# A long convolution with a spectral mixer: where the matrix of the modes is loaded

## The chip, the cores and the metric

The kernel runs on one core of a Trainium2 chip. The metric is the device time of one execution in microseconds (us); lower is better. Three runs of the kernel before took 382.86, 383.96 and 384.25 us, so the median is 383.96 us.

## The reference

What must be computed is a causal convolution over the sequence, followed by a mixer of 64 frequencies and a gated residual, for 8 batches of 5696 positions with 128 channels:

```python
def _attn_ref(x, h):                       # long convolution by FFT of twice the length
    L = 2 * S
    Yf = np.fft.rfft(x, n=L, axis=1) * np.fft.rfft(h, n=L, axis=0)[None, :, :]
    return np.fft.irfft(Yf, n=L, axis=1)[:, :S, :]

def _moe_ref(x, w_r, w_i, w_ch):
    X = np.fft.rfft(x, axis=1)             # only the first 64 frequencies are mixed
    Yr = einsum('bmd,mde->bme', Xr, w_r) - einsum('bmd,mde->bme', Xi, w_i)
    Yi = einsum('bmd,mde->bme', Xr, w_i) + einsum('bmd,mde->bme', Xi, w_r)
    u = x + np.fft.irfft(Y, n=S, axis=1)
    return u + np.maximum(u @ w_ch, 0.0)
```

## The kernel before

The transforms are matrix products. The sequence is split as 89 blocks of 64 positions. A first product over the 89 blocks gives 90 frequencies `k` (0 to 89) for each of the 64 places within a block; a second product, with the matrix `M`, transforms over the places; the result is multiplied with the filter's spectrum `Hs`; a third product, with `Wc`, goes back over the places, and its result `Zs` is stored to a scratch tensor in HBM. Much later a last stage loads it again, adds the mixer's part and writes the output.

The kernel writes out by hand, engine by engine, the order of all instructions: a recorder (class `Recorder`) takes each operation with the names of what it reads and writes, finds the semaphores that it must wait for, and appends it to its engine's list. Each engine, and each queue that issues transfers, works through its own list in order. All loads and stores named here are issued by SP (constants, `Hs`, `G`, stores of `Zs`) or by POOL (x, h and `M`).

The 8 batches are worked on in 4 pairs. The stages that matter here are:

- The tiles of the first pair (the loop over `a_tile(j, ...)` for j = 0 to 31, L668 to L674). Each tile is 8 matmuls of x (`Xin`) with the 90 frequencies and an eviction into `As`. Between them stand the 23 steps of the filter, `filter_tick(t, ...)` (L457), each for four frequencies: up to 16 matmuls of the filter's first transform `Ah` with `M`, and an eviction into `Hs`. After the steps 1, 5, 11, 17 and 22 (`HEND`), two transfers on SP copy the finished part of `Hs` from one half of the partitions to the other.
- The ticks of the first pair (`tick(g_, t)`, L646), t = 0 to 22, again of four frequencies each. A tick does `second` (matmuls with `M`), `products` (the multiplication with `Hs` on DVE, after an eviction by ACT), `third` of the tick two before (matmuls with `Wc`, eviction by ACT into one of ten buffers `Zs`/`Zt`, a 256 KB store to HBM issued by SP) and `modes_of` of the tick three before: small matmuls of `Zs` with `G`, which collect the 64 modes in one PSUM bank (the modes' matrix is `G`).
- In the ticks 2, 4, ... 16 a pair other than the last also issues the loads of the next pair's x (`x_load`, two transfers on POOL, 36 and 320 KB, into `Xt`), and in the ticks 9, 10, 13, 14, 17, 18, 20 and 22 (`XPLACE`) DVE copies what has landed into `Xin` (`x_place`, L356).
- After the ticks the tiles of the next pair follow, then its ticks, and so on.

`G` has 46 column groups of 128 (`NS`), one for each odd frequency and one that holds all even frequencies. It lies where `Ah` lay: group s takes the room of frequency s of `Ah`. It is loaded in six parts (`NG`) of eight groups (`GP`), five of 256 KB and one of 192 KB. A part may land only when the matmuls that read the same eight frequencies of `Ah` are done (the `after` of L480), and these belong to two steps of the filter. So in the kernel before `filter_tick` issues part i right behind step 2i + 1 (L477 to L480), on SP, behind any copy of `Hs` that the same step issues.

The matmuls of `modes_of` need part 0 from the first of them on (tick 3), and part i from frequency 16i - 1 on, whose `modes_of` stands in tick 4i + 2: part 1 in tick 6, part 2 in tick 10, part 5 in tick 22.

PE's instructions are not all on the chip at the start: while the kernel runs, a DMA queue of its own (q8 in the profile, "instruction") brings them in packets of 16 KB, over the same DMA engines.

## The time and the profile before

| | |
|---|---|
| median of three runs | 383.96 us |
| the profiled execution's own time | 384.32 us |
| its span, from the first to the last instruction | 382.2 us |
| mean granted TensorE clock | 0.988 |
| PE busy | 362.2 us (95%) |
| DVE busy | 307.4 us (80%) |
| ACT busy | 304.0 us (80%) |
| DMA queue q1 (issued by SP) | 67.73 MB, 51.5% of the 16 engines' time |
| DMA queue q0 (issued by POOL) | 35.43 MB, 44.2% |
| DMA queue q8 (instructions) | 42 packets, 0.69 MB, 0.7% |
| `G`: six issues on SP | 33.0 to 41.3 us, 9.8 to 11.8 us from issue to landing |
| `M`: six issues on POOL | 10.7 to 13.3 us, 18.1 to 28.7 us to landing |
| copies of `Hs` on SP | ten issues, 31.7 to 53.2 us, 3.5 to 11.7 us to landing |
| x for the second pair: 16 issues on POOL | 59.0 to 83.9 us, 2.7 to 7.2 us to landing |

Times within the execution count from its first instruction. The filter's steps run from 30.2 to 52.3 us, the first pair's ticks from 53.6 to about 93 us. "DMA share" is the mean busy share of the core's 16 DMA engines, where a value around 1 means that all are occupied all the time (packets can overlap a little, which gives values above 1). "issue" as the reason of an idle engine is time in which it waited for no semaphore that the profile shows.

### The profile page before, as it was taken

The page shows a single profiled execution, that of the slowest core. Times are in us where ns is not written, and L with a number is a line of the kernel's source. Part 1 is how long each engine was busy: PE and PEld are TensorE (multiplying, and loading weights), DVE is VectorE, ACT ScalarE, POOL GpSimd, SP SyncE. Part 2 cuts the span into 40 slices and gives each one's busy share as a digit, 9 for nine tenths or more (in the row PEclk, how much of TensorE's full clock was granted, in tenths as well). Part 3 has the DMA queues.
Part 4 walks back from the last instruction along what each step waited for, and adds up shares of the span by engine and source line. Part 5 has one row for each costly group of instructions (what it writes and reads, how often), then busy time and mean ns, then how long its engine had stood idle before and what let it go on. Part 6 is the DMA issues. An engine that isn't in the chain of part 4 may idle for free.

```text
span 382.2 us, 12483 instructions
## 1 busy us (share of the span) xinstructions
PE 362.2 (95%) x5372; PEld 284.0 (74%) x5372; DVE 307.4 (80%) x334; ACT 304.0 (80%) x497; POOL 81.9 (21%) x133
## 2 busy tenths in 40 slices
PE   7999789999989999989999899999999999989994
PEld 7998666666866667856667766668898988877873
DVE  6879678998998998989998888766347776766876
ACT  1269579999989998989998899994566777766785
POOL 8400003230652220832313010429100000000000
PEclk9999899999999999999999999998999999999998
DMA  7999978999899997999996379999999999999869
GB/s 146 195 282 370 239 180 159 242 240 276 89 150 204 234 255 213 119 131 235 246 272 144 39 238 365 322 328 383 397 406 403 409 401 411 409 399 377 346 267 358
DMA packets 83985, 103.94 MB, mean 272 GB/s; under 512 B 22062, under 2 KB 68910, under 8 KB 80450
## 3 DMA queue, kind: packets, MB, share of 16 engines
q1 hardware_dynamic: 59643, 67.73, 51.5%
q0 software_dynamic: 24288, 35.43, 44.2%
q8 instruction: 42, 0.69, 0.7%
q14 instruction: 12, 0.10, 0.1%
HBM read 70.61 MB, written 51.12 MB: 319 GB/s over the span
## 4 chain that ended last, share of the span: by engine, by line
PE 78%; ACT 9%; DMA 5%; DVE 5%; issue 2%; SPq 0%; DVEq 0%
PE ps L320 78%; ACT As L310 7%; DMA ZT0b<-zscr 5%; DVE As L314 2%; DVE U L594 1%; ACT R L832 1%; ACT UT L308 1%; DVE O L833 1%; DMA F<-cF 0%; DVE UT L312 0%; ACT XT L310 0%; SPq L317 0%; PE ps L786 0%; DVE Os L833 0%; DVEq L105 0%
## 5 line engine op out<-in xcount | busy, mean ns | idle before, releaser
L320 PE MATMUL ps<-U,Wc 128*128 128x512 f16 (+1 forms) x368 | 94.4, 376 | 0.0
L602 DVE TENSOR_TENSOR U<-Xs,Hs 128x2048 f16<-128x2048 f16 (+1 forms) x68 | 80.6, 1188 | 10.7 <-ACT Xs L308 9.6
L308 ACT CAST Xs<-ps 128x1024 f16<-128x1024 f32 (+1 forms) x72 | 69.5, 971 | 7.0 <-PE ps L320 4.8
L833 DVE TENSOR_TENSOR O<-ps,R 128x512 f32<-128x512 f32 x81 | 52.5, 686 | 22.1 <-ACT R L832 14.7
L308 ACT CAST Zs<-ps 128x512 f16<-128x512 f32 (+1 forms) x126 | 66.1, 605 | 0.0
L832 ACT ACTIVATE R<-ps 128x512 f32<-128x512 f32 x96 | 51.0, 573 | 16.0 <-PE ps L320 15.5
L314 DVE TENSOR_SCALAR As<-ps 128x720 f16<-128x720 f32 x64 | 53.5, 880 | 8.5 <-PE ps L320 7.2
L320 PE MATMUL ps<-F,Xin 128*128 128x180 f16 x512 | 54.6, 253 | 4.3 <-issue 2.6
L310 ACT ACTIVATE As<-ps 128x720 f16<-128x720 f32 (+1 forms) x68 | 49.0, 773 | 11.9 <-PE ps L320 10.7
L320 PEld LDWEIGHTS ps<-F,Xin 128*128 128x128 f16 x512 | 46.1, 156 | 11.4 <-DVE As L314 3.1
L320 PE MATMUL ps<-WI,UT 128*128 128x256 f16 x360 | 52.0, 279 | 1.8 <-DVE O L833 1.7
L320 PE MATMUL ps<-As,M 64*128 64x128 f16 x1440 | 48.6, 217 | 4.5 <-DVE U L594 3.5
L320 PEld LDWEIGHTS ps<-U,Wc 128*128 128x128 f16 x368 | 28.2, 97 | 28.9 <-ACT Zs L308 6.8
L320 PEld LDWEIGHTS ps<-As,M 64*128 64x128 f16 x1440 | 40.3, 94 | 10.3 <-DVE U L594 4.2
L317 POOL DMA_DIRECT2D Xt<-in_x_dram x48 | 25.0, 525 | 104.7 <-PE ps L320 104.0
L602 DVE TENSOR_TENSOR U<-ps,Hs 128x2048 f16<-128x2048 f32 x20 | 45.7, 2284 | 0.0
L308 ACT CAST UT<-ps 128x712 f16<-128x712 f32 x40 | 30.0, 752 | 18.3 <-PE ps L320 17.3
L320 PEld LDWEIGHTS ps<-WI,UT 128*128 128x128 f16 x360 | 39.2, 152 | 5.7 <-ACT R L832 2.6
L320 PE MATMUL ps<-IBs,C 128*128 128x356 f16 x128 | 39.9, 321 | 0.7
L320 PEld LDWEIGHTS ps<-G,Zs 128*128 128x128 f16 x492 | 27.0, 96 | 12.6
L308 ACT CAST Zt<-ps 128x512 f16<-128x512 f32 (+1 forms) x58 | 31.0, 605 | 0.0
L320 PE MATMUL ps<-G,Zs 128*128 128x2 f16 (+2 forms) x492 | 30.3, 191 | 0.0
(87 smaller groups left out, 503.8 us busy)
## 6 DMA issues: line engine op xcount, KB each, us to landing
out_dram<-O SPq DMA_DIRECT2D x39, 512.0 KB, 11.8
zscr<-Zs SPq DMA_DIRECT2D x60, 256.0 KB, 6.9
Xt<-in_x_dram POOLq DMA_DIRECT2D x24, 320.0 KB, 6.9
zscr<-Zt SPq DMA_DIRECT2D x28, 256.0 KB, 6.3
W<-wscr POOLq DMA_DIRECT2D x4, 1024.0 KB, 7.7
M<-cM POOLq DMA_DIRECT2D x5, 720.0 KB, 20.5
ZT0a<-zscr SPq DMA_DIRECT2D x3, 1024.0 KB, 15.1
Xr<-in_x_dram POOLq DMA_DIRECT2D x8, 320.0 KB, 14.0
```

Source lines behind the costliest of these rows:

```text
L308: R.add(e, lambda h_: h_.copy(dst, src), reads, writes, after=after)
L310: R.add(e, lambda h_: h_.activation(dst, src, COPY, scale=scale), reads, writes, after=after)
L314: R.add(e, lambda h_: h_.tensor_scalar_mul(dst, src, scale), reads, writes, after=after)
L317: R.add(eng, lambda h_: h_.dma_start(dst, src), reads, writes, ring=ring, after=after)
L320: R.add("tensor", lambda h_: h_.matmul(o, l, r, start=st, stop=sp), reads, writes)
L594: R.add("vector", lambda e, b=b, s_=s_: e.tensor_tensor(bass.AP(u_s[i], b * 512, [[2048, P], [1024, 2], [1, n * D]]), s_, hv, MULT), [tok, ...
L602: R.add("vector", lambda e: e.tensor_tensor(uv, src, hv, MULT), bk + [("h", t, 0), ("h", t, 1, 0), ("h", t, 1, J)], [("u", i)])
L832: R.add("scalar", lambda e: e.activation(rv, src_r, RELU), bk, [("r", i % NR)], after=once(("r", i % NR), G_ALL + XTT + [("y", 0), ("y", 1 ...
L833: R.add("vector", lambda e: e.tensor_tensor(ov, src_u, rv, ADD), bk + [("r", i % NR)], [key + (h_,)], after=once(key, old))
```

## The change

The six loads of `G` leave `filter_tick` and become a function `load_g(i)` with the same transfer, the same queue (SP), the same ring of semaphores and the same condition on `Ah`. It is called in the loop over the ticks: in the first pair, ahead of the ticks 0, 2, 4, 6, 8 and 10.

```diff
@@ filter_tick
-        if t % 2 and t // 2 < NG:
-            s0, s1 = t // 2 * GP, min(t // 2 * GP + GP, NS)
-            dma("sync", g_sb[:, s0 * P:s1 * P], bass.AP(c_g, s0 * P, [[GW, P], [1, (s1 - s0) * P]]), "c", (),
-                [("g", t // 2)], after=[("ag", k) for k in range(s0, s1)])
+
+    def load_g(i):
+        s0, s1 = i * GP, min(i * GP + GP, NS)
+        dma("sync", g_sb[:, s0 * P:s1 * P], bass.AP(c_g, s0 * P, [[GW, P], [1, (s1 - s0) * P]]), "c", (),
+            [("g", i)], after=[("ag", k) for k in range(s0, s1)])
...
     for g_ in range(NP):
         for t in range(NT + LM if g_ + 1 == NP else NT):
+            if g_ == 0 and t % 2 == 0 and t // 2 < NG:
+                load_g(t // 2)
             tick(g_, t)
```

The lists of PE, DVE, ACT and POOL hold the same instructions in the same order as before. On SP the ten copies of `Hs` now stand one after another; parts 0 and 1 of `G` follow behind the last of them, ahead of the first store of `Zs`; then two stores, part 2, two stores, part 3, two stores, part 4, two stores, part 5, and the remaining stores.

## The prediction

> **What bounds the kernel now.** I began with the chain of work that ended last, since it says what each stretch of the 382.2 us is made of, and looked at the two stages that the change touches.

> ```profile
> 2.58 31.37 PE ps L320 x416
> ...
> 33.97 7.91 PE ps L320 x190
> 41.88 2.58 issue
> 44.46 4.53 PE ps L320 x82
> ...
> 55.52 37.69 PE ps L320 x580
> ```

> The columns are start, length and what. PE is on the path nearly throughout, but at 41.88, in the stage in which `G` is loaded, there is a hole of 2.58 us with no semaphore behind it. PE's timeline shows that it is no wait of a tile: a tile is eight matmuls on one PSUM slot, and here it breaks off after six.

> ```profile
> 41.19 0.70 PE L320 MATMUL ps<-F,Xin 128*128 128x180 f16 x6
> 44.46 0.32 PE L320 MATMUL ps<-F,Xin 128*128 128x180 f16 x2 [2.58 <-issue]
> ```

> What was missing is instructions. The DMA view for 35 to 41.6 us has no packet of the instruction queue; the one for 41.6 to 44.46 us has one, beside a q1 (`G` and `Hs`) that fills the engines:

> ```profile
> q1 hardware_dynamic: 247, 0.65, 102.9%
> q8 instruction: 1, 0.02, 2.8%
> ```

> In the trace's packets this fetch runs from 41.64 to 42.94. How late was it? PE has 10,861 records; at this stop it stands at record 1217, at the only other hole of this kind (341.36, 1.48 us, again with a fetch just begun) at 10083, 35 fetches later: 253 records a packet. If a packet is asked for when the one before it has been used up, this one was asked for at record 964, at 36.7 us, and waited 5.0 us for its turn. Fetches while the DMA was almost idle (57.6 to 58.2 us) waited 0.6, those behind q0 alone (`Xr` and `M`, at 13 and 23 us) 1.7, those behind the long q1 of the last stage 7 to 10. So a fetch waits for a part of what is queued, most of all on q1.

> The hole costs more than itself. Three windows: a usual one, the hole, and 90 matmuls of the same shapes after it.

> ```profile
> 34.31:37.77 3.46, 3.46 (x90) 2.90 (x84) 3.19 (x5) 3.13 (x6) 0.00 (x0) 1.00 1.03 302
> 41.88:44.46 2.58, 0.00 (x1) 0.00 (x0) 0.79 (x1) 0.00 (x1) 0.00 (x0) 1.00 1.04 230
> 45.28:49.98 4.70, 4.58 (x90) 4.01 (x85) 3.14 (x5) 3.58 (x6) 0.00 (x0) 0.64 0.78 192
> ```

> The last three columns are granted clock, DMA share and GB/s. Behind the hole the clock was cut (0.51 from 45.28 to 48.77), and the same work took 4.70 instead of 3.46 us: 1.24 us more. The hole is worth 2.58 + 1.24 = 3.8 us. The clock records have no cut behind the hole of 1.48 us at 341.

> Then the stage that `G` moves into:

> ```profile
> 57.00:59.00 2.00, 2.00 (x39) 1.38 (x39) 1.97 (x3) 2.00 (x4) 0.00 (x0) 1.00 0.05 12
> 60.00:62.00 2.00, 2.00 (x44) 1.48 (x43) 1.79 (x2) 1.89 (x4) 0.07 (x1) 1.00 0.85 66
> 62.00:76.00 14.00, 14.00 (x225) 9.27 (x224) 12.81 (x11) 13.78 (x23) 4.14 (x8) 1.00 1.05 237
> 76.00:90.00 14.00, 14.00 (x218) 9.15 (x217) 13.79 (x13) 13.78 (x23) 3.11 (x6) 1.00 1.07 247
> ```

> From 57 to 59 us the DMA rests (share 0.05); from 62 to 90 all 16 engines are full, and PE, DVE (13.79 of 14) and ACT are full as well. The four ticks of 7.0 us hold, on each DMA engine, two x loads (5 packets of 0.323 us each and a little) and four stores (32 packets of 0.027): about 7.1 us. There is no room left.

> **The change, part by part.** *Six SP issues go from 33 to 41 us.* SP waits there for the filter's evictions and delays nobody; freed issue time is worth 0. `Hs` copies are next in the queue; the first pair needs the early ones from 53.6 us on and they landed by 46.3, so their earlier landing is worth 0. `M`'s last part landed at 42.0 and is first used at about 47.6: also 0.

> *1.4 MB less for the DMA engines while PE's fetch waits.* On the engine that lags most, the packets before the fetch are the rest of `M`, two `Hs` copies and part 0; part 1 landed after it (44.5). At 230 GB/s a part of 256 KB is 1.1 us. Without part 0 the fetch would start at 40.5; if part 1 as well was in its way on shared engines and ports, at 39.4. PE resumed 2.8 us after the fetch began, so it would resume at 43.3 or 42.2, 1.4 or 0.3 us after it runs dry at 41.88. I take the middle, a hole of 0.9 us, and no cut of the clock, since 1.48 us did not bring one: gain 2.58 - 0.9 + 1.24 = 2.9 us. Bounds: 0, if the `Hs` copies issued at 35.3 and 35.8 take the place of `G` ahead of the fetch, and 3.8, if the hole goes altogether.

> [...]

> *Parts 0 and 1 behind the last `Hs` copy.* SP ends that issue at 54.7. An `Hs` copy (3.5 to 4.1 us there) and a store (2.7 us at 58.2) put part 0's landing between 57.4 and 58.8; the last `Hs` packets end at 56.9 and the DMA is idle after. The first matmul with `G` stands at 58.7 to 58.9. I take 0, with 0.9 us as the upper bound. It would hold all of PE's list, `second` of tick 4 first.

> *Parts 2 to 5 between the stores* (issued at some 60.5, 63.7, 67.5 and 70.7; needed from tick 10 on, 71 us, 78, 85 and 92, so each has over 9 us). SP spends 0.6 us on each, and its stores have buffers for ten ticks: 0. But on each DMA engine a part is 8 packets of at least 0.084 us, the median of 2 KB packets: 0.67 us, for all four 2.5 us into a stretch that is full. What is late next is the x load. By the trace's landings the eight loads are done 0.5 to 4.4 us before DVE copies them; the sixth is the tightest, 84.07 against this copy:

> ```profile
> 84.53 0.68 DVE L356 COPY Xin<-Xt 89x2048 f16<-89x2048 f16 x1
> ```

> If x waits its turn for everything in front, it comes 2.5 us later and DVE, which has no slack, loses 2.5 - 0.46 = 2.0 us. If x is served in turns with the stores, it loses 0. Nearest row: on the engine that is furthest behind, stores land up to 3.7 us after the median engine (84.10 against 80.43), but x loads 1.8 (84.07 against 82.28). So x bears about 0.45 of a backlog: 1.1 us, less 0.46 of slack, 0.6 us. Bounds 0 and 2.0.

> **The sum.** 384.32 - 2.9 + 0.6 = 382.0 for the profiled execution, which lies 0.36 above the median: 381.7 against 383.96.

> **The rivals.** (1) *The fetch is as late as before*: the `Hs` copies fill the place of `G`, or the queue was never the cause. For it: the two copies issued at 35.3 and 35.8 us carry as many bytes each as a part of `G` (256 KB); against it, the fetches behind short queues, which were early. Alone 384.0; with x late by 0.6 us, 384.6. (2) *Both halves come out middling*: a hole of 1.5 to 2 us that still cuts the clock, or a gain of 2 us paid back by x: 382.5 to 384. (3) *Slower: the second pair's x is late.* All of `G`'s 2.5 us falls on x, DVE's copies in ticks 14 to 18 stall by 2.0 us, PE and ACT with them, while the hole stays: 386.0. For it: the DMA share of 1.05 to 1.07 and slacks of 0.46, 0.65 and 0.84 us at three copies. Against it: x bears less than half of a backlog now. It decides from a delay of 0.46 us on, and beats the gain where the hole stays. A second fetch stall in the ticks would come on top; the fetch at 85.0 us now ends 3.2 us before it is needed. (4) *The change does not move what it says*: excluded, the SP list shows it.

> **How the numbers follow.** 0.5% (1.92 us) is about what a measurement of this kernel can tell from no change. Forecast (hole mostly gone, x little late; 380.2 to 382.0): 0.46. Rivals 1 and 2, within 0.5%: 0.28. Rival 3 and what adds to it, over 385.9: 0.26; it gets that much because every engine is full where `G` goes and the hole is one place only. Range 379.9 to 386.3: 383.96 less the full 3.8 with 0.3 to spare, up to the full 2.0 with the hole kept and some of part 0's wait. For the likeliest case alone it is 380.2 to 382.0.

> **What would show it.** Right: no idle PE over 1.5 us with reason "issue" near 42 us, a clock of 1.0 from 45 to 49, the ticks starting about 3 us earlier, and 37 to 39 us from the first U product to the tiles. Wrong: the hole of over 2 us still there; DVE waiting for `Xt` in the ticks; PE waiting for `G` at tick 3; or the hole moved to another fetch.

## The result, and the profile after

| | before | after |
|---|---|---|
| median | 383.57 us (20 runs, 381.32 to 386.53) | 381.39 us (20 runs, 380.40 to 385.21) |
| ratio after to before | | 0.9947, 95% interval 0.9926 to 0.9968 |
| the profiled execution | 384.32 us, span 382.2 | 385.21 us, span 383.1 |
| mean granted clock in it | 0.988 | 0.985 |
| hole near 42 us | 2.58 us | 0.83 us |
| tick 0 of the first pair starts | 53.60 us | 51.12 us |
| first pair's tick 0 to second pair's tick 0 | 54.52 us | 54.51 us |

The change makes the kernel 0.53% faster, about 2 us; 381.7 us was predicted and 381.39 measured. The execution that was profiled is the slowest of the 20, slower than the profile of before, so its span can't be set against the other. Its stages can. The chain of waits of after (start, length, what), in the stages of the prediction's first fence:

```profile
34.40 8.05 PE ps L320 x190
42.45 0.83 issue
43.28 0.68 PE ps L320 x18
...
53.04 37.69 PE ps L320 x580
```

The hole is 0.83 us where it was 2.58, and the ticks' uninterrupted stretch of PE begins 2.48 us earlier and is exactly as long as before (37.69), although the six parts of `G` are now loaded in it. PE's timeline of after shows that the stop is the same one, after six of eight matmuls:

```profile
41.75 0.70 PE L320 MATMUL ps<-F,Xin 128*128 128x180 f16 x6
43.28 0.32 PE L320 MATMUL ps<-F,Xin 128*128 128x180 f16 x2 [0.83 <-issue]
```

The 8 us around it in windows (length; PE, PEld, DVE, ACT, POOL with their instructions; granted clock, DMA share, GB/s), first before, then after:

```profile
41.00:49.00 8.00, 5.42 (x106) 4.74 (x98) 3.93 (x6) 4.00 (x7) 0.00 (x0) 0.79 0.91 215
```

```profile
41.00:49.00 8.00, 7.00 (x197) 5.92 (x196) 6.83 (x10) 6.40 (x11) 0.00 (x0) 1.00 0.70 152
```

In the same 8 us PE does 197 instructions instead of 106, at a clock of 1.00 instead of 0.79: the hole is shorter and no cut of the clock follows it. The DMA engines move 152 instead of 215 GB/s.

What the ticks pay for the six loads is in the waits of after from 53 to 91 us (what waited for what: us in total, times, longest):

```profile
PE ps L320 <- DVE U L595: 0.9, 1, 0.9
...
PEld ps L320 <- DMA G<-cG: 0.3, 1, 0.3
```

The first line stands in before too, with the same 0.9. The second is new: part 0 is late for tick 3 by 0.3 us, and the stretch is none the longer for it (37.69). No line has DVE waiting for `Xt`.

Why was this execution slow as a whole? Its chain of waits has two transfers late in the last pair that the chain of before does not have:

```profile
243.00 11.81 DMA zscr<-Zt
...
265.98 15.82 DMA ZT4b<-zscr
281.85 14.05 PE ps L320 x182
```

A store of `Zt` took 11.81 us to land. POOL's load `ZT1a` waits for that store, the later loads of POOL's list stand behind `ZT1a`, and PE then waited 2.3 us for `ZT4b`. In both profiles this store is issued 0.11 us ahead of POOL's load `ZT0a`, so it is no new neighbourhood. A repeat of after (the run a0 below) shows the wait, with a store of `Zs` that took 11.68 us in that place. Another (a1) does not: its store took 9.52 us, but `ZT4b` landed in time at 278.86 us. The late store is issued 166 us after the last part of `G` has landed (77.12 us). How many of the 20 runs have the wait is not known.

### The profile page after: what moved, and what is told of

It reads as the page before. It is cut to its first block, busy times and chain, and to the rows that moved or that the text cites. A ratio compares the mean times of both kernels' runs of the same rounds, so it can differ in the third digit from the quotient of the medians.

```text
span 383.1 us, 12483 instructions
## 1 busy us (share of the span) xinstructions
PE 362.8 (95%) x5372; PEld 283.6 (74%) x5372; DVE 305.9 (80%) x334; ACT 303.7 (79%) x497; POOL 81.5 (21%) x133
## 3 DMA queue, kind: packets, MB, share of 16 engines
HBM read 70.61 MB, written 51.12 MB: 318 GB/s over the span
## 4 chain that ended last, share of the span: by engine, by line
PE 65%; DMA 12%; ACT 10%; DVE 5%; POOL 5%; issue 2%; POOLq 0%; DVEq 0%
PE ps L320 65%; ACT As L310 6%; DMA Xr<-in_x_dram 5%; DMA ZT4b<-zscr 4%; DMA zscr<-Zt 3%; DVE As L314 2%; POOL Xr L317 2%; DVE U L595 1%; ACT R L835 1%; ACT UT L308 1%; ACT Zs L308 1%; DVE O L836 1%; POOL ZT1b L508 0%; POOL ZT3b L508 0%; POOLq L105 0%
## 5 line engine op out<-in xcount | busy, mean ns | idle before, releaser
L320 PE MATMUL ps<-U,Wc 128*128 128x512 f16 (+1 forms) x368 | 94.5, 376 | 0.0
L314 DVE TENSOR_SCALAR As<-ps 128x720 f16<-128x720 f32 x64 | 53.6, 880 | 7.7 <-PE ps L320 6.2
L320 PE MATMUL ps<-F,Xin 128*128 128x180 f16 x512 | 53.7, 250 | 3.4 <-DVE Xin L356 0.9
L320 PEld LDWEIGHTS ps<-F,Xin 128*128 128x128 f16 x512 | 45.3, 155 | 10.7 <-DVE As L314 3.1
L320 PE MATMUL ps<-WI,UT 128*128 128x256 f16 x360 | 52.6, 282 | 0.5 <-DVE O L836 0.4
L320 PE MATMUL ps<-As,M 64*128 64x128 f16 x1440 | 48.6, 217 | 4.5 <-DVE U L595 3.5
L320 PEld LDWEIGHTS ps<-U,Wc 128*128 128x128 f16 x368 | 28.2, 97 | 28.8 <-ACT Zs L308 6.8
L320 PEld LDWEIGHTS ps<-As,M 64*128 64x128 f16 x1440 | 40.3, 94 | 10.3 <-DVE U L595 4.1
L320 PEld LDWEIGHTS ps<-WI,UT 128*128 128x128 f16 x360 | 39.6, 152 | 4.5 <-issue 1.9
L320 PE MATMUL ps<-IBs,C 128*128 128x356 f16 x128 | 40.5, 326 | 0.7
L320 PEld LDWEIGHTS ps<-G,Zs 128*128 128x128 f16 x492 | 27.0, 96 | 12.7 <-DMA G<-cG 0.3
L312 DVE CAST UT<-ps 128x712 f16<-128x712 f32 x24 | 21.3, 890 | 11.7 <-PE ps L320 11.7
```

Of the source, the lines that this page charges most:

```text
L312: R.add(e, lambda h_: h_.tensor_copy(dst, src), reads, writes, after=after)
L314: R.add(e, lambda h_: h_.tensor_scalar_mul(dst, src, scale), reads, writes, after=after)
L320: R.add("tensor", lambda h_: h_.matmul(o, l, r, start=st, stop=sp), reads, writes)
```

## The experiments

The table gives for every kernel one profiled execution. Its times count from the first matmul of the filter's transform (`Ah`, at 30.1 to 30.8 us in all of them), since executions differ by some tenths in when x first arrives. "Fetch" is the start of the packet with the instructions missing at the hole, and "hole" is the stop near 42 us; e6 and d7 have further stops, which are told there. The last column is against before measured beside it; b0 and a0 are single runs.

```
                       fetch  hole   clock cut   tick 0  ticks'   sum    ratio to before
                              us     near 45     starts  length          (95% interval)
before                 11.44  2.58   3.4 us      23.40   54.52   77.92
b0 before again        11.97  2.75   3.4 us      23.82   54.50   78.32
after                  10.09  0.83   none        20.48   54.51   74.99   0.9947 (0.9926-0.9968)
a0 after again         10.35  1.32   none        20.84   54.48   75.32
a1 after again         10.48  1.52   3.4 us      22.22   54.51   76.73   0.9943 (0.9910-0.9975)
e1 parts 0, 1 moved    10.79  2.20   none        22.05   54.48   76.53   1.0000 (0.9972-1.0028)
e2 parts 2-5 moved     11.42  2.62   3.4 us      23.18   54.49   77.67   1.0019 (0.9991-1.0047)
e3 G loaded twice      12.12  3.30   6.8 us      24.82   54.51   79.33   1.0011 (0.9989-1.0033)
e4 8 copies in ticks   10.53  1.46   none        20.97   58.09   79.06   1.0057 (1.0033-1.0081)
e5 G on POOL           11.84  2.94   none        22.46   54.48   76.94   0.9987 (0.9972-1.0002)
e6 Hs after 11         7.48   0      6.8 at 58   20.27   60.31   80.58   1.0044 (1.0026-1.0062)
c5 Hs after 5          9.11   0      none        19.71   54.51   74.22   0.9916 (0.9882-0.9949)
c7 Hs after 7          7.26   0      none        19.54   54.67   74.21   0.9895 (0.9851-0.9939)
d7 before, Hs after 7  8.90   0.51   none        20.72   55.30   76.02   0.9955 (0.9926-0.9985)
```

"Ticks' length" is from the first pair's tick 0 to the second pair's, "sum" where the second pair's ticks start. The diffs of e1 to e4, e6, c5 and c7 are against after, those of e5 and d7 against before; "..." stands for lines left out.

**b0: before, once more.** Is the hole an accident of the one profiled execution?

> The kernel before, unchanged, for a second profile. Theory (an instruction fetch of PE waits behind the queued transfers): the hole near 42 us stands again, 2 to 3 us long, at the same place in PE's order (after six matmuls of a tile), with the clock cut behind it. If the hole is an accident of the one profiled execution, it is missing or elsewhere, and then the gain of the change has another cause.

It came again, 2.75 us, at the same two matmuls, with the clock cut behind it:

```profile
45.46 0.46 PE L320 MATMUL ps<-F,Xin 128*128 128x180 f16 x2 [2.75 <-issue]
```

Its time was 385.09 us. The hole belongs to the kernel.

**a0: after, once more.**

> The changed kernel, unchanged, for a second profile, since its first was the slowest of its 20 runs (385.21 us). Theory: the hole near 42 us is again under 1.5 us and the clock is not cut; the first pair's ticks start some 2.5 us earlier than before; the 2.3 us that PE waited in the first profile at 279.5 us for the load of ZT4b are shorter or gone, since they have nothing to do with G. If that wait is a price of the change, it is there again.

The hole was 1.32 us with no cut, and tick 0 started 20.84 us after the filter's first matmul; the run took 383.6 us, with the wait for `ZT4b` (2.2 us) here again. The early gain is the same as in the first profile, so the loss late in both is a separate matter.

**e1: only parts 0 and 1 leave the tiles.** By the prediction they are what the fetch waited behind.

```diff
@@ filter_tick, at its end
+        if t % 2 and t // 2 in (2, 3, 4, 5):
+            load_g(t // 2)
...
-            if g_ == 0 and t % 2 == 0 and t // 2 < NG:
+            if g_ == 0 and t % 2 == 0 and t // 2 in (0, 1):
                 load_g(t // 2)
```

> Parts 0 and 1 of G are loaded in the ticks 0 and 2, parts 2 to 5 among the tiles as before. Theory (the fetch that PE asks for at about 37 us is behind what was issued on SP before 35 us, of G only parts 0 and 1): the hole is about as short as in the changed kernel, 0.5 to 1.3 us, and the time falls by about 2 us, ratio 0.994 to 0.996. Rival (the sum of bytes in flight counts, so four parts of six left in place keep the hole): hole 1.7 to 2.6 us, ratio 0.997 to 1.000.

```profile
44.63 0.32 PE L320 MATMUL ps<-F,Xin 128*128 128x180 f16 x2 [2.20 <-issue]
```

The hole is 2.20 us, far from the 0.83 to 1.52 of after, and the time is that of before (383.84 against 383.62, ratio 1.0000). The theory that only what stands ahead of the fetch counts has fallen. The fetch did start 0.9 us earlier than in the mean of the two profiles of before, but PE resumed 3.26 us after its start, where it was 2.83 and 2.89 there. This profile's sum (76.53) would promise 1.6 us; the profiled execution is the fastest of its 12 runs (382.24) and had no cut near 45 us. Its mean granted clock is 0.993, that of the eleven others 0.982 to 0.990. A cut of 3.41 us at a granted clock of 0.50, as the clock records of before have it at 45.36 us, takes about 0.0045 from the mean over 380 us, so the others were cut for longer; where is not known.

**e2: only parts 2 to 5 leave the tiles.**

```diff
@@ filter_tick, at its end
+        if t % 2 and t // 2 in (0, 1):
+            load_g(t // 2)
...
-            if g_ == 0 and t % 2 == 0 and t // 2 < NG:
+            if g_ == 0 and t % 2 == 0 and t // 2 in (2, 3, 4, 5):
                 load_g(t // 2)
```

> Parts 0 and 1 stay among the tiles, parts 2 to 5 are loaded in the ticks 4 to 10. Theory: the hole is as in the kernel before, 2.2 to 2.8 us with the clock cut, ratio 0.998 to 1.002. Rival (the sum of bytes counts): hole 0.8 to 1.8 us, ratio 0.994 to 0.997.

```profile
44.72 0.46 PE L320 MATMUL ps<-F,Xin 128*128 128x180 f16 x2 [2.62 <-issue]
```

The hole stays at 2.62 us. So neither group by itself gives the gain: against the mean of the two profiles of before (11.70) the fetch starts 0.9 us earlier with parts 0 and 1 gone, 0.3 with parts 2 to 5 gone, and 1.4 (the mean of three profiles of after) with all gone. The 0.3 is not clear of chance, since the two profiles of before are 0.5 us apart.

**e3: `G` is loaded in both places.** This keeps the hole and puts the whole load on the ticks.

```diff
@@ filter_tick, at its end
+        if t % 2 and t // 2 in range(NG):
+            load_g(t // 2)
...
```

> Every part of G is loaded twice: among the tiles as before, and again in the ticks as in the changed kernel. So it has the hole of the kernel before and the added transfers in the ticks. Theory (the gain comes from the hole alone and the transfers in the ticks cost nothing on the path): the hole of 2.2 to 2.8 us is back, the ticks are as long as before (37.7 us from the second tick's matmuls to the tiles), ratio 0.998 to 1.002. Rival (the transfers in the ticks cost something that the gain hid): ticks 0.5 to 2 us longer, ratio 1.002 to 1.006.

```profile
45.47 0.46 PE L320 MATMUL ps<-F,Xin 128*128 128x180 f16 x2 [3.30 <-issue]
```

The hole is back, the gain is gone (384.17 against 383.30 us), and the ticks' length is 54.51 us. The six loads in the ticks cost nothing measurable, and what the change gains comes from the tiles alone.

**e4: three loads' worth in the ticks.** How much more could they carry? To after, eight copies of 256 KB are added, two with each of four `G` loads, into a scratch tensor that nothing reads.

```diff
+    gd = nc.dram_tensor("gscr", [8 * P, 1024], F16, kind="Internal")
...
             if g_ == 0 and t % 2 == 0 and t // 2 < NG:
                 load_g(t // 2)
+                for i in range(2 if 4 <= t <= 10 else 0):
+                    dma("sync", bass.AP(gd, (t - 4 + i) * P * 1024, [[1024, P], [1, 1024]]), bass.AP(c_g, i * 1024, [[GW, P], [1, 1024]]), "c")
```

> The changed kernel with two more transfers of 256 KB behind each of the parts 2 to 5 on SP (copies from G's constant to a scratch tensor in HBM that nobody reads): three times the bytes in the full stretch, some 5 to 7 us more for each DMA engine. Theory (x is served in turn with SP's queue, the stores bear the backlog): x lands at most 1 us later, the ticks grow by under 1 us, ratio to the kernel before 0.994 to 0.998. Rival (x waits for all that was issued before it): x lands 5 us and more late, DVE waits for it, ticks 4 to 6 us longer, ratio 1.004 to 1.012.

The ticks grew by 3.6 us and the kernel is slower than before (385.63 us). But x is not what was late. The waits of this kernel from 60 to 110 us, and its chain of waits in the same stretch:

```profile
ACT Zt L309 <- DMA zscr<-Zt: 3.7, 2, 3.3
```

```profile
79.36 10.04 DMA zscr<-Zt
```

ACT, which evicts into `Zt`, had no free buffer of the ten: a store took 10.04 us on the path, up to 12.7 elsewhere. The big x loads still landed within 7.8 us (7.2 at most in before), and no copy of DVE waited for them. So x came in time and the stores bore the backlog, as the theory had it, though no record shows in what order the queues were served; the price of eight more loads, under 1 us by the theory, was wrong. The time that the rival gave came about by another mechanism.

**e5: before, with `G` issued by POOL.** Is it q1, the queue of SP, that the fetch waits for?

```diff
-            dma("sync", g_sb[:, s0 * P:s1 * P], bass.AP(c_g, s0 * P, [[GW, P], [1, (s1 - s0) * P]]), "c", (),
+            dma("gpsimd", g_sb[:, s0 * P:s1 * P], bass.AP(c_g, s0 * P, [[GW, P], [1, (s1 - s0) * P]]), "c", (),
                 [("g", t // 2)], after=[("ag", k) for k in range(s0, s1)])
```

> The kernel before with the six loads of G issued by POOL at the same places, so that they stand in queue q0 behind the rest of M and not in q1 between the copies of Hs. Same bytes, same time, other queue. Theory (a fetch waits for little of q0 and much of q1): the hole shrinks to 0 to 1.3 us, ratio 0.992 to 0.997. Rival (any transfer in flight holds the fetch, or the bandwidth does): hole 2 us or more, ratio 0.998 to 1.002.

```profile
44.76 0.32 PE L320 MATMUL ps<-F,Xin 128*128 128x180 f16 x2 [2.94 <-issue]
```

The hole is as long as ever. For `G` the queue made no difference here: with it on q0 the fetch started at 11.84 us, with it on q1 at 11.44 and 11.97, while with `G` in the ticks it starts 1.4 us earlier. In this execution the clock was not cut, though the hole is longer than that of before:

```profile
44.40:47.80 3.40, 2.98 (x82) 2.62 (x82) 2.20 (x3) 2.52 (x5) 0.00 (x0) 1.00 0.71 202
```

**e6: after, with the `Hs` copies only behind steps 11 and 22.** If everything in flight holds the fetch, the copies of `Hs` must too.

```diff
-    HEND = [1, 5, 11, 17, NT - 1]
+    HEND = [11, NT - 1]
```

> The changed kernel with the filter's steps after which Hs is copied cut from five (1, 5, 11, 17, 22) to two (11, 22): the four Hs transfers that were issued before PE's fetch at about 37 us come after it. Theory: with nothing of q1 ahead of it, the fetch starts within 2 us of its request and the hole of 0.8 us goes to 0: ratio to the kernel before 0.991 to 0.994, the fastest so far. Rival (the rest of M holds the fetch): hole as in the changed kernel, ratio 0.994 to 0.996. The larger copies could hold a later fetch (the next is asked for at 43 us) and open a hole there.

The fetch started 7.48 us after the filter's first matmul, 2.8 us earlier than in the mean of after, and the hole at 42 us is gone. A short one has opened at the next fetch, which now falls into the time of the first large copy (40.5 to 50.5 us). PE's timeline of this kernel:

```profile
48.14 0.61 PE L320 MATMUL ps<-Ah,M 64*128 64x64 f16 x30 [0.71 <-issue]
```

The last copy, moreover, now has 11 steps' worth in one piece and stands in SP's queue ahead of part 0 of `G`, and the first matmul with `G` waits:

```profile
59.26 0.72 PE L320 MATMUL ps<-G,Zs 128*128 128x128 f16 x8 [3.01 <-DMA G<-cG]
```

The clock was cut for 6.8 us from 58.2 us on, while PE still stood, the ticks took 60.31 us, and the kernel is slower than before (385.39 us). It is the wait at tick 3 that the prediction bounded with 0.9 us: 0.3 in after, 3.01 here.

**a1: after, timed again.**

> The changed kernel, unchanged, timed a second time beside the kernel before, with a third profile. In both earlier profiles POOL's load of ZT1a waited for a store of Zt that had queued behind POOL's own loads, ZT4b then landed at 281.7 us and PE stood 2.35 us for it; in the kernel before that store went ahead of them. If this is a draw from execution to execution, the median of this kernel is again about 0.9945 of the kernel before and this profile may or may not show the wait; if the change brings it, the wait is there in every profile and the ratio is 0.997 to 1.000.

The ratio is 0.9943: the result repeats. Its profile has the hole at 1.52 us, and this time a cut behind it. PE's timeline and the windows of a1:

```profile
43.64 0.32 PE L320 MATMUL ps<-F,Xin 128*128 128x180 f16 x2 [1.52 <-issue]
```

```profile
44.40:47.80 3.40, 3.40 (x68) 2.95 (x63) 2.29 (x3) 2.22 (x5) 0.00 (x0) 0.58 0.14 36
```

So the same kernel gets the cut in one execution and not in the next, and its ticks start 1.4 and 1.7 us later than in the two others (22.22 against 20.84 and 20.48); 0.2 and 0.7 us of that is the longer hole itself.

**c5 and c7: after, with the first `Hs` copy behind step 5, or step 7,** and the last ones in small pieces as they were.

```diff
-    HEND = [1, 5, 11, 17, NT - 1]
+    HEND = [5, 11, 17, NT - 1]
```

```diff
-    HEND = [1, 5, 11, 17, NT - 1]
+    HEND = [7, 11, 17, NT - 1]
```

> The changed kernel without the early copy of Hs behind step 1 (copies behind the steps 5, 11, 17, 22): of what SP issues before PE's fetch is asked for at about 37 us only the copies of 35 us are left, which arrive with it. Theory (whatever is in flight holds the fetch, so half a megabyte less lets it start 1 us earlier): the hole of 1.1 to 1.6 us shrinks to 0 to 0.4 us and no new one opens; tick start 0.8 to 1.4 us earlier than in the changed kernel; ratio to the kernel before 0.990 to 0.994. Rival (the rest of M holds it): no change against the changed kernel, 0.9945.

> As the run before, with the first copy behind step 7 (7, 11, 17, 22): nothing of SP is in flight when the fetch is asked for. Theory: no hole at 42 us. The next fetch, asked for at about 41.5 us and needed at 46.5, now stands behind a copy of eight steps (1 MB, 4 to 5 us): a hole of 0 to 1 us at 47 us, as with two copies only (0.9 us there). Ratio to the kernel before 0.990 to 0.996, at best that of the run before.

Neither has a hole at 42 us, c7 none at the next fetch either. The windows of c7:

```profile
41.00:49.00 8.00, 7.61 (x201) 6.48 (x198) 7.51 (x11) 7.05 (x12) 0.00 (x0) 1.00 0.86 202
```

The DMA share is higher there than in after (0.86 against 0.70): the copies are only later, not fewer bytes. c5 took 380.78 us, c7 380.60 (ratio 0.9895), the fastest kernel of this study, ahead of both before and after by its median. Its six runs do not separate it from c5, nor, by the intervals alone, from after.

**d7: before, with the copies as in c7,** so `G` stays among the tiles.

```diff
-    HEND = [1, 5, 11, 17, NT - 1]
+    HEND = [7, 11, 17, NT - 1]
```

> The kernel before (G among the tiles) with the copies of Hs behind the steps 7, 11, 17 and 22, as in the fastest kernel so far. It tells whether late copies alone do what the two edits do together. Theory (every transfer in flight adds to the fetch's wait): with parts 0 and 1 of G in the place of the copies the fetch is earlier than in the kernel before by 1 to 2.5 us; hole 0.3 to 1.8 us, ratio 0.993 to 0.998, slower than late copies with G in the ticks. Rival (the copies alone hold it): no hole, ratio 0.988 to 0.992. Rival (G alone holds it): hole of 2.5 us and more.

```profile
42.48 0.32 PE L320 MATMUL ps<-F,Xin 128*128 128x180 f16 x2 [0.51 <-issue]
48.40 0.61 PE L320 MATMUL ps<-Ah,M 64*128 64x64 f16 x30 [0.72 <-issue]
55.71 0.45 PE L320 MATMUL ps<-As,M 64*128 64x128 f16 x10 [0.46 <-issue]
```

Three short holes instead of a long one, the second and third at the next two fetches, which now meet `G` and the delayed copies. The third lies in the ticks, which are 0.8 us longer. With 382.15 us (ratio 0.9955) moving the copies alone gains, within the intervals, as much as moving `G` alone.

## Why the prediction came out

**What bounds: right.** That the hole is a fetch of instructions held up by transfers was read from the trace of before, and the experiments show it: fewer bytes in flight, in any of three ways (`G` away, the copies later, both), start the fetch earlier (at 10.09 to 10.48, 8.90 and 7.26 us, against 11.44 and 11.97), and the hole is shorter or gone. PE resumed 2.5 to 3.3 us after the start of the fetch at all 14 stops of this kind before 60 us (table, e6, d7), where the prediction had 2.8. When a packet is asked for, no record shows. That this one was asked for at 36.7 us, 6.5 us after the filter's first matmul, is the author's estimate from the count of PE's records, and the runs fit it: with both out of the way (c7) the fetch started at 7.26, which is 0.8 us later, near the 0.6 reckoned in the same way for the fetch of 58.18 us, with the DMA almost idle (share 0.05 from 57 to 59 us). Of the waiting time by this estimate in before (11.70 less 6.5, 5.2 us) `G` accounts for 1.4 us (after), the early copies of `Hs` for 2.8 (d7), and both for 4.4 (c7).

The second stop on which the prediction rested, at 341 us, is not of this kind. PE waits there for a semaphore that DVE's `O` releases at 342.81. PE's timeline of before:

```profile
342.95 0.64 PE L320 MATMUL ps<-WI,UT 128*128 128x256 f16 x4 [1.31 <-DVE O L833]
```

So the 253 records a packet were counted from a wrong mark, and came out nearly right by luck. The three stops of d7 are at PE's records 1217, 1473 and 1731, 256 and 258 apart. Counted with 256, the same estimate has the fetch of 41.64 asked for at 36.6 us, and its wait of 5.0 us stands; but for the fetches of the last stage that were read as waiting 7 to 10 us it gives 4.9 to 6.5 (those from 296 to 351 us).

**The gain of 2.9 us: right in two executions of three.** The residual hole was put at 0.9 us; it was 0.83, 1.32 and 1.52. Tick 0 started 2.9 us earlier in after than in before and 3.0 in a0 than in b0, but only 1.4 earlier in a1 than the mean of the two (23.61), because there the clock was cut. The mean of the three starts is 21.18, a gain of 2.4 us. That agrees with the median's 0.53% of 383.57, 2.0 us.

The prediction had no cut, "since 1.48 us did not bring one". Its mark was the misread stop at 341 us, but the conclusion fits the traces: no hole of up to 1.46 us (e4) brought one. The clock records show why the length of a hole alone does not decide. In all 14 profiles every cut starts a whole number of steps of 3.41 us after the first record of the clock (7.81 us in before, whose cut at 45.36 comes 11 steps later), and, the one at the end of each kernel left aside, lasts one or two steps. What goes with a cut is PE's idle time within one such step. The step of a1 ahead of its cut, and the next; then the two steps that share the hole of e5 (the columns are those of the windows above):

```profile
40.42:43.84 3.42, 1.90 (x44) 1.49 (x42) 2.41 (x3) 1.69 (x3) 0.00 (x0) 1.00 0.78 186
43.84:47.25 3.41, 3.41 (x75) 2.92 (x74) 1.98 (x3) 2.13 (x3) 0.00 (x0) 0.50 0.32 86
```

```profile
39.89:43.31 3.42, 1.94 (x46) 1.57 (x44) 2.41 (x3) 1.94 (x4) 0.12 (x1) 1.00 1.02 267
43.31:46.72 3.41, 1.96 (x62) 1.72 (x63) 1.25 (x2) 1.44 (x3) 0.00 (x0) 1.00 0.85 232
```

PE is idle for 1.52 us in the step of a1, and for 1.48 and 1.46 in those of e5. Over all profiles, with the clock at full speed and the end of the kernel left aside, a step with 1.52 us or more of idle PE was followed by a cut (1.52 in a1, 1.94 in e6, 2.04 in e3, 2.26 in e2, 2.36 in after at 282 us, 2.51 in b0, 2.52 in before), and no step with 1.48 us or less was, but for one place: at 258 to 266 us every profile has a cut behind a step with at most 0.2 us of idle PE, and what brings that one is open. A hole of 0.9 us is less than what stood ahead of any of these cuts; that of a1 was 0.6 us longer, all of it in one step, and there the cut came.

**The reason for it: partly wrong.** The prediction held parts 0 and 1 to be what counted, since part 1's end lay behind the fetch. By e1 they are worth 0.9 us of fetch time of the 1.4, and no measurable time. It also said "most of all on q1", and e5 shows the same hole with `G` on q0. The rival that the copies of `Hs` fill `G`'s place has its core confirmed: they were the larger part of the wait, and the hole at 42 us is gone only where they come late as well (c5, c7 and e6). But they did not move up so far as to keep the fetch where it was.

That part 1 was in the fetch's way "on shared engines and ports" stood behind the earlier of the prediction's two times for it, 39.4 us. No run shows a port, or which transfers a fetch has to wait out. In place of the 1.1 and 2.2 us by which the two estimates had it start earlier, the runs showed 0.9 with parts 0 and 1 gone (e1) and 1.4 with all six gone.

**Parts 0 and 1 behind the last copy: right.** Taken as 0 with a bound of 0.9 us; 0.3 us of a weight load's wait, absorbed. That this wait can decide is shown by e6.

**The loss of 0.6 us by late x: mis-sized, it is 0.** The term let x bear a share of the backlog, by how much later it lands on the engine furthest behind. In after the first three of the eight loads landed 0.1 to 0.9 us later after the start of tick 0 than in before, and the other five 0.3 to 0.8 us earlier. No copy waited: the one that was tightest, with 0.46 us, had 1.24 us of slack, and the least of the eight is 1.14. The DMA view of 62 to 90 us, before and then after (what, queue, count, size, median us to landing):

```profile
zscr<-Zs SPq DMA_DIRECT2D x9, 256.0 KB, 7.3
Xt<-in_x_dram POOLq DMA_DIRECT2D x7, 320.0 KB, 7.0
zscr<-Zt SPq DMA_DIRECT2D x7, 256.0 KB, 6.2
```

```profile
zscr<-Zs SPq DMA_DIRECT2D x8, 256.0 KB, 8.4
zscr<-Zt SPq DMA_DIRECT2D x8, 256.0 KB, 6.9
Xt<-in_x_dram POOLq DMA_DIRECT2D x6, 320.0 KB, 6.5
```

The stores take 0.7 to 1.1 us longer, x 0.5 us less. The stores have ten buffers, so nobody waits, until the load is tripled as in e4. A DMA share of 1.05 to 1.07 was read as "no room left"; but in the same two windows after moved 291 and 275 GB/s (share 1.10 and 1.09) where before had 237 and 247, and the ticks took the same time.

**The sum.** 2.4 us of gain and no loss came where 2.9 and 0.6 had been put: 2.3 predicted for the balance, 2.2 measured between the medians. The two errors nearly cancel: a hole taken as 0.9 us, where the mean of the three is 1.2 and one of them brought a cut, and a loss of 0.6 that did not come. That the number is so much better than its terms is luck.

**Not settled.** Why the fetch started later where more was in flight (7.26 us in c7, 11.44 in before, 12.12 in e3) could not be read from the traces. The wait for `ZT4b`, where 2.3 us of the profiled execution went, occurs in two profiles of after out of three and in neither of before. None of the nine other kernels shows it, and five of these load all of `G` in the ticks as well (e3, e4, e6, c5, c7); the store issued 0.11 us ahead of `ZT0a` took 3.8 to 4.9 us there. Since the time of a1 repeats the ratio with 0.9943 too, the wait is not taken as the change's price; but no kernel was made that takes it away or provokes it in before, so that is argued, not shown.

## What to carry to other kernels

An idle stretch with no semaphore behind it, in the middle of an unrolled group, is worth a look at the instruction queue: loads and copies that could run later can hold up a fetch. Here `G` did so on either queue (holes of 2.58 and 2.75 us on q1, 2.94 on q0), and the shares nearly add up: 1.4 us of the fetch's time for `G`, 2.8 for the copies, 4.4 for both. Where bulk transfers may go is decided less by the DMA share than by what waits for them: here the stores, with ten buffers, took up 1.4 MB at no measurable cost, while eight more loads of 256 KB cost 3.6 us. And a transfer that is moved past others in its queue is measured by its first use, as e6's 3.01 us show.
